# Holding one load of x, one set of output products and one early store in the planner's order of a fused attention and state-space kernel

## The chip, the cores and the metric

The kernel runs on one core of a Trainium2 chip. The metric is device time in microseconds (us) of one execution. Five engines matter: TensorE (PE, with its weight loads shown as PEld), ScalarE (ACT), VectorE (DVE), GpSimd (POOL), and SyncE (SP), which here only issues DMAs.

## The reference

The input x has 2048 rows of 448. Two branches are computed from it and mixed by a gate per row:

```python
x = A_x
g = _sigmoid((x * gate_w).sum(-1, keepdims=True))
a = _A_ref(x, A_wq, A_wk, A_wv, A_wo)
b = _B_ref(x, B_A_re, B_A_im, B_B_re, B_B_im, B_C_re, B_C_im, B_log_dt, B_Dskip)
return g * a + (1 - g) * b
```

Branch A is attention with 16 query heads of 28 and one shared key and value head: scores of 2048 x 2048 per head, softmax, the product with v, and an output product with wo. Branch B is a long convolution of each of the 448 channels with a kernel K of 2048 taps, K being a sum over 256 complex modes, plus a skip term.

## The kernel before, in words

The rows of x are taken as four query chunks of 512 rows, and each chunk's 16 heads as four groups of four heads, so there are 16 items i = 0 to 15 (chunk i // 4, group i % 4). Each item has 16 key tiles times 4 heads, 64 score tiles of 128 x 512; there are 1024 score tiles in all. They are worked on in 410 sets, by turns three tiles and two: `qk` (L1298) puts a set's scores into PSUM banks 0 to 4, either from `qT` with K of 29 rows (L1311) or from the masked copy `qM` with 128 rows (L1334), and ACT takes the exponential of the set in one instruction (L1366) into a ring of tiles `expT`. `pv` multiplies four such tiles with v (L1385) into `psB`, and after 16 key tiles `norm` (L1140) copies the sums to `acc` (L1146), fetches the denominators by three small round trips through POOL's DMA queue (denT, R_scratch, rdenB), and writes the normalised heads to `onT` (L1158).

`qproj(i)` (L860) makes the queries of item i: four matmuls of `xT` with Wq (L870), an absolute maximum on DVE (L876), one more matmul (L879), a copy to `qT` (L882), and four DMAs on POOL's queue to `qM`. `xT` holds one query chunk. After the last group of a chunk, at i = 3, 7 and 11, `qproj` also loads the next chunk of x from the DRAM scratch `XS` into `xT`, 448 KB on POOL's queue. The one at i = 7 brings the third chunk, which `qproj(8)` to `qproj(11)` read.

When a chunk's four groups are normalised, `outp(qc, tt)` (L1122) forms the output products of one of its four tiles of 128 rows: four matmuls with Wo (L1128) into one bank, and `fold` (L1134) adds them, times the gate, to the result `O` on DVE (L1137). qc = 2 is the third chunk.

Branch B runs in the shade of this. `masters` and `tables` build tables of powers on DVE, `kgen(c)` (L1002) for c = 0 to 13 multiplies them into 32 channels of K (L1022), copies them out (L1034) and writes them to the DRAM scratch `KP` by POOL's queue. `tload` brings them back as Toeplitz tiles, about 1.1 MB in four DMAs on SP's queue, into one of five buffers (three in `T`, two in `U` once `U` is used up), and two such loads feed one of the 28 convolutions. `conv(c)` (L1074) has 128 small matmuls, 32 planner operations of four (L1089, kept in `self.cm[c, 0..31]`), a scaling copy (L1099), 16 transposing matmuls (L1110) and an addition into `O` (L1119). `stores` writes the first 320 columns of the first three chunks early, one DMA per chunk on SP's queue.

The order on each engine is not the order of the code. Every operation is given to a planner (`Prog`) with an engine, an assumed duration, its data dependencies and a priority `pr` (smaller goes first: score sets 0, the load of x 1, convolutions 1.6, output products 1.58, query products 1.5). `schedule` (L180 on) is a list scheduler: it keeps a clock per engine, takes at each step the operation that can start first, by priority where times tie, and so fixes each engine's sequence. Output products, convolutions, `kgen` and query products share two PSUM banks (5 in `psS`, and `psX`), handed out as locks. The planner also counts PE's instructions and keeps to a time for the fetching of each block of 256. Its gaps on PE are filled with matmuls that only keep the array busy (L1293).

`pg.after[i] = j` makes operation i wait, in the plan, until j is placed:

```python
for i, d in self.after.items():
    if d not in ops[i].deps:
        need[i] += 1
        succ[d].append(i)
```

It does not enter `deps`, and only `deps` become semaphore waits in `waits` and `emit`. The early stores use this too: `STORES` names three score sets, and store qc is held in the plan until the first scores of its set are placed. After that it still waits, by semaphore, for the four tiles of `O` that it writes out.

Of the kernel before, what the change touches and what calls it, by code (L numbers as in the profile page):

```python
# [44 lines left out]
WARM = 64  # L45
NEWQ = 15
LASTQ = 13
STORES = (338, 341, 362)
EARLY = 20
PAIRS = 3  # L50
OUTB = (None, 4, 1, 2)
# [10 lines left out]
class Buf:  # L62
    def __init__(self, handle):
        self.h = handle
        self.rs = handle[:].ap[0][0]
# [17 lines left out]
def dram(t, off, dims):  # L83
    return bass.AP(tensor=t.tensor, offset=t.offset + off, ap=[list(d) for d in dims])
# [308 lines left out]
def el(n, rate=0.96, fix=68):  # L393
    return fix + n / rate
# [14 lines left out]
class Kernel:  # L409
    def __init__(self, nc, ins, out):  # L410
        self.nc, self.ins, self.out = nc, ins, out
        self.es = ExitStack()

    def sb(self, name, cols, dt):
        return Buf(self.es.enter_context(self.nc.sbuf_tensor(name, [P, cols], dt)))
# [4 lines left out]
    def build(self):  # L420
        nc = self.nc
        with self.es:
            self.pg = Prog(nc, self.es)
            self.alloc()
            self.consts()
            self.loads()
            self.prep_x()
            self.prep_params()
            self.prep_u()
            self.prep_gate()  # L430
            self.main()
            self.pg.schedule()
            with nc.Block() as block:
                self.pg.emit(block)
# [425 lines left out]
    def qproj(self, i):  # L860
        pg = self.pg
        qc, g = i // 4, i % 4
        s = i % 2
        X = ("qx", i)
        G = self.grp()
        px = lambda: G.v(0, P, 0, [[1, 512]])

        pr = 0.2 if i == 0 else 1.45 if i < 4 else 1.5
        for T in range(NT):
            pg.op("pe", lambda e, T=T: e.matmul(  # L870
                px(), self.Wq.v(0, DT, T * 512 + g * 128, [[1, 128]]),
                self.xT.v(0, DT, T * 512, [[1, 512]]), start=(T == 0), stop=(T == 3),
                tile_position=(0, 0), skip_group_check=True), 226,
                rd=["Wq"] + self.xk(0) + (["kap"] if i == 1 else []), wr=[X, ("q", s)], pr=pr, lock=G if T == 0 else None)
        av = self.qT.v(0, P, 512 * s, [[1, 512]])
        pg.op("dve", lambda e: e.tensor_reduce(  # L876
            av, G.v(0, P, 0, [[1, 512], [1, 1]]), AX.X, ALU.max, apply_absolute_value=True), el(512),
            rd=[X], wr=[("q", s)], pr=pr)
        pg.op("pe", lambda e: e.matmul(px(), self.Wb.v(0, P, 0, [[1, P]]), av, start=False, stop=True,  # L879
                                       tile_position=(0, 0), skip_group_check=True), 230,  # L880
              rd=["Wb", ("q", s)], wr=[X], pr=pr)
        o = pg.op("dve", lambda e: e.tensor_copy(self.qT.v(0, P, 512 * s, [[1, 512]]), px()), el(512),  # L882
                  rd=[X], wr=[("q", s)], pr=pr, unlock=G)
        if i == 0:
            self.qc0 = o.i
        if i in (3, 7, 11):
            pg.dma([(self.xT.v(0, DT, 0, [[1, XQ]]), dram(self.XS, qc * DT * XQ, [[XQ, DT], [1, XQ]]))],
                   (112, 4096), "xl", rd=[("XS", qc + 1)], wr=self.xk(0), pr=1, eng="pool", extra=9000)
        if True:
            pg.dma([(self.qM.v(32 * h, 32, s * XQ + 512 * h, [[1, 512]]), self.qT.v(32 * h, 32, 512 * s, [[1, 512]]))  # L890
                    for h in range(4)], (128, 1024), f"qm{s}", rd=[("q", s)], wr=[("qM", s)], pr=0, eng="pool", extra=4500)
# [230 lines left out]
    def outp(self, qc, tt):  # L1122
        pg = self.pg
        X = ("ox", qc, tt)
        G = self.grp()
        px = lambda: G.v(0, P, 0, [[1, D]])
        for g in range(4):
            pg.op("pe", lambda e, g=g: e.matmul(  # L1128
                px(), self.onT.v(0, P, g * 512 + 128 * tt, [[1, 128]]), self.Wo.v(0, P, g * D, [[1, D]]),
                start=(g == 0), stop=(g == 3), tile_position=(0, 0), skip_group_check=True), 200,  # L1130
                rd=["Wo"] + [("on", gg) for gg in range(4)], wr=[X], pr=1.58, lock=G if g == 0 else None)
        self.fold(qc, tt, px, 0, D, [X], unlock=G)

    def fold(self, qc, tt, px, off, n, rd, unlock=None):  # L1134
# [130 lines left out]
    def main(self):  # L1265
# [32 lines left out]
        def qk(s):  # L1298
# [58 lines left out]
            self.prevset = o.i  # L1357
            if s in STORES:
                self.hold.append(o.i)
# [121 lines left out]
```

## Time and profile before

| what | us |
|---|---|
| median of 3 runs | 501.96 (500.3 to 503.63) |
| the profiled execution | 504.37 |
| its span, first to last instruction | 502.6 |
| ACT busy | 484.9 |
| PE busy | 479.3 |
| DVE busy | 455.6 |

The span holds a start of some 22 us, in which x is transposed and the first queries are made, then the 410 exponentials from 21.8 to 495.6 us, and a tail of 7 us for the last products and stores. PE's busy time contains 150 filling matmuls of 385 ns (L1293). All three engines are close to full, so one reads the profile for the places where ACT, the fullest, is idle.

### The profile page before, as it was taken

The numbers are of one execution on the slowest core, as the hardware profiler recorded it, in microseconds if no ns is written. First come the engines' busy times: TensorE is split into PE (matmuls) and PEld (weight loads), VectorE is DVE, ScalarE is ACT, GpSimd is POOL, SyncE is SP. The second block draws the span as 40 slices with busy tenths as digits, with TensorE's granted clock in tenths as the row PEclk, the third lists the DMA queues.
The fourth block names the chain that finished last, engine by engine and source line by source line (L and its number), as shares of the span: only waits on it lengthen the run. The fifth ranks groups of instructions, "written<-read, shape, count | busy, mean of one in ns | idle before, by whom it ended". The sixth has DMA issues, their size and how long they took to land.

```text
span 502.6 us, 17345 instructions
## 1 busy us (share of the span) xinstructions
PE 479.3 (95%) x7643; PEld 210.2 (42%) x7643; DVE 455.6 (91%) x867; ACT 484.9 (96%) x436; POOL 146.3 (29%) x282
## 2 busy tenths in 40 slices
PE   8899999999999999799999999999999999999997
PEld 6432233343443434344343343543534344444453
DVE  6999999999999999899999999999999999896213
ACT  6999999999999999899999999999999999899995
POOL 2102044234143433214306052520513424143110
PEclk9999999999999999999999999999999999899999
DMA  8997695928438566992943951499693776739742
GB/s 243 323 188 186 121 155 131 270 61 256 142 81 269 154 182 112 280 215 42 296 98 52 287 159 65 120 265 320 128 326 48 215 238 186 232 103 306 226 163 69
DMA packets 152423, 91.86 MB, mean 183 GB/s; under 512 B 84538, under 2 KB 148332, under 8 KB 152348
## 3 DMA queue, kind: packets, MB, share of 16 engines
q1 hardware_dynamic: 143370, 81.21, 60.8%
q0 software_dynamic: 8704, 9.41, 7.6%
q8 instruction: 60, 0.98, 0.8%
q14 instruction: 15, 0.12, 0.1%
q10 hardware_dynamic: 274, 0.14, 0.1%
HBM read 73.61 MB, written 5.23 MB: 157 GB/s over the span
## 4 chain that ended last, share of the span: by engine, by line
ACT 81%; PE 10%; DMA 1%; issue 1%; SPq 0%
ACT expT L1366 81%; PE psS L1311 2%; PE psS L1334 2%; DMA T<-KP_scratch 1%; PE psB L1385 1%; PE psS L1089 1%; PE psS L1224 1%; PE psB L1293 1%; PE psX L1022 1%; PE psB L1287 1%; PE psX L1089 0%; SPq L158 0%; PE psS L1022 0%; PE psS L870 0%; PE psX L870 0%
## 5 line engine op out<-in xcount | busy, mean ns | idle before, releaser
L1366 ACT ACTIVATE expT<-psS 128x1536 bf16<-128x1536 f32 (+1 forms) x410 | 465.1, 1390 | 6.3 <-PE psS L1334 3.0
L963 DVE TENSOR_TENSOR tab<-tab,mbf 128x512 bf16<-128x512 bf16 (+4 forms) x140 | 139.5, 1000 | 0.0
L1311 PE MATMUL psS<-qT,kT 29*128 29x512 bf16 x684 | 96.3, 387 | 10.3 <-ACT expT L1366 5.2
L1385 PE MATMUL psB<-expT,vaug 128*32 128x512 bf16 x1000 | 100.5, 392 | 0.1
L1334 PE MATMUL psS<-qM,kT 128*128 128x512 bf16 x316 | 95.4, 385 | 1.5 <-ACT expT L1366 0.4
L158 POOL DMA_DIRECT2D KP_scratch<-kstg x104 | 57.4, 559 | 84.0 <-DVE kstg L1034 76.5
L978 DVE TENSOR_TENSOR tab<-tab 128x256 bf16<-128x256 bf16 (+4 forms) x140 | 76.9, 574 | 0.0
L1385 PEld LDWEIGHTS psB<-expT,vaug 128*32 128x32 bf16 x1000 | 25.6, 93 | 73.3 <-issue 71.5
L158 POOL DMA_DIRECT2D qM<-qT x64 | 32.4, 513 | 61.7 <-DVE qT L882 39.9
L1311 PEld LDWEIGHTS psS<-qT,kT 29*128 29x128 bf16 x684 | 23.7, 91 | 63.6 <-ACT expT L1366 49.3
L1293 PE MATMUL psB<-ident,one 128*128 128x512 bf16 x150 | 48.8, 385 | 0.0
L158 POOL DMA_DIRECT2D rdenB<-R_scratch x60 | 30.9, 520 | 51.3 <-DMA R_scratch<-denT 51.1
L1089 PE MATMUL psS<-T,U 128*26 128x128 bf16 (+3 forms) x1792 | 40.0, 223 | 0.9 <-DMA T<-KP_scratch 0.9
L1089 PEld LDWEIGHTS psS<-T,U 128*26 128x26 bf16 (+3 forms) x1792 | 30.9, 106 | 14.7 <-issue 9.2
L1089 PE MATMUL psX<-T,U 128*32 128x128 bf16 (+3 forms) x1472 | 34.4, 222 | 2.2 <-issue 2.2
L158 POOL DMA_DIRECT2D denT<-acc x15 | 10.8, 718 | 88.0 <-DVE acc L1146 88.0
L992 DVE TENSOR_TENSOR tab<-tab,tmp 128x1984 bf16<-128x1984 bf16 x28 | 32.3, 1186 | 0.1
L1089 PEld LDWEIGHTS psX<-T,U 128*32 128x32 bf16 (+3 forms) x1472 | 25.8, 106 | 15.8 <-issue 11.3
L1334 PEld LDWEIGHTS psS<-qM,kT 128*128 128x128 bf16 x316 | 19.0, 97 | 28.2 <-ACT expT L1366 19.1
L986 DVE TENSOR_TENSOR tmp<-tmp,mq 128x64 bf16<-128x64 bf16 (+4 forms) x70 | 25.5, 365 | 0.1
L909 DVE TENSOR_TENSOR msq<-seedz 128x512 f32<-128x512 f32 (+1 forms) x40 | 24.6, 615 | 0.0
L1022 PE MATMUL psX<-tab 128*64 128x128 bf16 x544 | 22.6, 224 | 1.3 <-issue 1.0
(187 smaller groups left out, 483.8 us busy)
## 6 DMA issues: line engine op xcount, KB each, us to landing
T<-KP_scratch SPq DMA_DIRECT2D x204, 272.0 KB, 5.2
U<-KP_scratch SPq DMA_DIRECT2D x20, 272.0 KB, 5.5
rdenB<-R_scratch POOLq DMA_DIRECT2D x60, 64.0 KB, 3.7
U<-cst SPq DMA_DIRECT2D x1, 3584.0 KB, 23.8
qM<-qT POOLq DMA_DIRECT2D x64, 32.0 KB, 3.8
tab<-in_A_x_dram SPq DMA_DIRECT2D x4, 448.0 KB, 5.5
O<-in_A_x_dram SPq DMA_DIRECT2D x16, 112.0 KB, 4.6
O<-cst SPq DMA_DIRECT2D x1, 1792.0 KB, 9.5
```

The lines of the kernel that those rows point to most:

```text
L158: return [e.dma_start(o, i, **kw) for o, i in pairs]
L963: mul = lambda e, o, a, b: e.tensor_tensor(o, a, b, ALU.mult)
L978: vo(lambda e, dv=dv, tv=tv, k=k: e.tensor_tensor(dv, dv, tv, ALU.add if k else ALU.subtract), n, [kt[k], kd[k]], [kd[k]], 1.92 if lv else ...
L986: vo(lambda e, w=w, lv=lv: e.tensor_tensor(rho.v(0, P, (32 - 2 * w) * 2, [[64, 32], [2, w], [1, 2]]), rho.v(0, P, (32 - w) * 2, [[64, 32], ...
L992: vo(lambda e, k=k: e.tensor_tensor(tab.v(0, P, FM + k * FP + 2, [[64, 32], [2, 31], [1, 2]]), tab.v(0, P, lm + k * PL + 62, [[64, 32], [- ...
L1022: r = e.matmul(G.v(64 * u, 64, 128 * k, [[1, 128]]), tab.v(0, P, lo + comp * PL + cg * 64 + u, [[2, 64]]), tab.v(0, P, fo, [[64, 2], [mo - ...
L1089: r = e.matmul(ps.v(32 * j, 32 - m0, 128 * k, [[1, 128]]), self.U.v(0, P, (4 * gi + j) % UA // 2 * 128 + 2 * (2 * m0 + par) + j % 2, [[4, ...
L1293: return e.matmul(t.v(0, P, off, [[1, 512]]), self.one.v(0, P, 2, [[0, P]]), self.ident.v(0, P, 0, [[0, 4], [1, P]]), start=b != 6, stop=b ...
L1311: r = e.matmul(self.psS.v(0, P, 512 * b, [[1, 512]]), kT.v(32 * h, DH + 1, 128 * kt, [[1, 128]]), qT.v(32 * h, DH + 1, 512 * (i % 2), [[1, ...
L1334: return e.matmul(self.psS.v(0, P, 512 * b, [[1, 512]]), kT.v(0, P, 128 * kt, [[1, 128]]), self.qM.v(0, P, (i % 2) * XQ + 512 * h, [[1, 51 ...
L1366: o = pg.op("act", lambda e: e.activation(expT.v(0, P, 512 * es[0], spread(es, n)), self.psS.v(0, P, 512 * bs[0], spread(bs, n)), AF.Exp, ...
L1385: r = e.matmul(self.psB.v(32 * h, 32, 0, [[1, 512]]), vaug.v(0, P, 32 * kt, [[1, 32]]), expT.v(0, P, 512 * ring[t], [[1, 512]]), start=(kt ...
```

## The change

Three things are held later in the plan. The load of the third chunk of x is not placed before the first operation of convolution 9. The first matmul of each of the four output products of the third chunk (and with it the three that follow) is not placed before the last operation of convolution 21. The third early store is tied to score set 366 and not 362. The two holds are noted in a list while the operations are made, as the operations of the convolutions don't exist yet, and go into `pg.after` just ahead of `schedule`. No instruction is added or removed by the text of the change; the planner works its order out anew.

```diff
-STORES = (338, 341, 362)
+STORES = (338, 341, 366)
...
     def __init__(self, nc, ins, out):
         self.nc, self.ins, self.out = nc, ins, out
         self.es = ExitStack()
+        self.held = []
...
             self.main()
+            for i, c in self.held:
+                self.pg.after[i] = self.cm[c]
             self.pg.schedule()
...
         if i in (3, 7, 11):
             pg.dma([(self.xT.v(0, DT, 0, [[1, XQ]]), dram(self.XS, qc * DT * XQ, [[XQ, DT], [1, XQ]]))],
                    (112, 4096), "xl", rd=[("XS", qc + 1)], wr=self.xk(0), pr=1, eng="pool", extra=9000)
+            if i == 7:
+                self.held.append((pg.ops[-1].i, (9, 0)))
...
                 rd=["Wo"] + [("on", gg) for gg in range(4)], wr=[X], pr=1.58, lock=G if g == 0 else None)
+            if qc == 2 and g == 0:
+                self.held.append((pg.ops[-1].i, (21, 31)))
         self.fold(qc, tt, px, 0, D, [X], unlock=G)
```

## The prediction

> **What bounds the kernel now.** I read the page of the profile first (busy shares, the chain that ended last, the DMA queues), then the windows of 12.56 us for where ScalarE is not full, then the timeline of those windows, then the landings of the loads of T.
>
> ```profile
> span 502.6 us, 17345 instructions
> PE 479.3 (95%) x7643; PEld 210.2 (42%) x7643; DVE 455.6 (91%) x867; ACT 484.9 (96%) x436; POOL 146.3 (29%) x282
> q8 instruction: 60, 0.98, 0.8%
> ACT 81%; PE 10%; DMA 1%; issue 1%; SPq 0%
> ```
>
> ScalarE's exponentials (ACT) are 81% of the chain, so what leaves ACT idle in the main loop is what can be gained. The windows (columns: window, length, then busy time and count for PE, PEld, DVE, ACT, POOL; granted clock, DMA share, GB/s) show where that is:
>
> ```profile
> 201.00:213.60 12.60, 9.66 (x205) 4.04 (x192) 10.22 (x16) 10.44 (x10) 3.27 (x6) 0.93 0.95 280
> 213.60:226.20 12.60, 12.47 (x285) 6.08 (x283) 11.52 (x22) 11.75 (x11) 1.99 (x4) 0.94 0.92 215
> 226.20:238.70 12.50, 12.33 (x208) 5.79 (x207) 12.50 (x32) 12.50 (x12) 5.28 (x9) 1.00 0.23 41
> ...
> 339.30:351.80 12.50, 11.54 (x208) 4.75 (x206) 11.32 (x23) 11.82 (x11) 0.72 (x1) 1.00 1.06 320
> ...
> 427.20:439.80 12.60, 11.45 (x245) 5.70 (x233) 10.84 (x26) 11.29 (x11) 1.74 (x4) 0.89 0.78 231
> 439.80:452.30 12.50, 12.40 (x245) 6.06 (x243) 11.87 (x16) 11.97 (x12) 5.09 (x9) 0.97 0.36 102
> ```
>
> ACT idles 2.16 + 0.85 = 3.01 us at 201 to 226, 0.68 at 339 to 352, 1.31 + 0.53 = 1.84 at 427 to 452: 5.53 us in all. Elsewhere between 75 and 490 it is full. DVE idles in the same three places, so its long chain moves up with them. The timeline of the first and third place:
>
> ```profile
> 200.30 0.56 POOL L158 DMA_DIRECT2D xT<-XS_scratch  x1 [2.01 <-PE psS L1089]
> 208.53 0.41 PE L1089 MATMUL psX<-T,U 128*26 128x128 bf16 x15
> 211.15 0.49 PE L1089 MATMUL psX<-T,U 128*30 128x128 bf16 x21 [2.20 <-issue]
> 212.50 1.02 ACT L1366 ACTIVATE expT<-psS 128x1024 bf16<-128x1024 f32 x1 [2.09 <-PE psS L1334]
> ...
> 427.31 2.55 SPq L158 DMA_DIRECT2D U<-KP_scratch  x4
> 430.33 2.60 SPq L158 DMA_DIRECT2D T<-KP_scratch  x4
> 432.98 0.60 SPq L158 DMA_DIRECT2D out_dram<-O  x1
> 434.77 0.31 PE L1022 MATMUL psX<-tab 128*64 128x128 bf16 x4
> 436.08 0.31 PE L1022 MATMUL psX<-tab 128*64 128x128 bf16 x4 [1.01 <-issue]
> ```
>
> Both PE gaps lie inside a group of matmuls and no semaphore ends them ("issue"). The trace's DMA packets name the cause: queue 8 carries 60 packets of 16,384 B, one per about 256 PE instructions, that is PE's own code. One began at 208.49 and took 1.14 us; PE went on 1.5 us after it landed (211.15 against 209.63). Another began at 433.60, landed at 434.74, and PE went on at 436.08. Counted in PE's instruction records (a fetch comes after 254 of them in the mean) these two were due at 205.2 and 429.2, so they waited 3.3 and 4.4 us before they began; by that count they are the two latest of the 60. In both cases loads of T filled the DMA engines (280 GB/s at 201 to 213). After both gaps the clock records show half clock for 3.41 us, which doubles the harm.
>
> A rule speaks against this reading: the Trainium skill, "Runtime: NRT & Kernel Launch", section "Instruction fetch mechanics", says that code is prefetched in 16 KiB blocks and that this is mostly hidden. The trace agrees on the size and differs on the hiding in 2 of 60 cases. By that rule the gaps are something else, the change would leave them, and the time is 502.0. That is rival 2.
>
> **The load of x, third chunk.** One DMA on POOL's queue (0.56 us there), 448 KB, whose 4096 B packets ran from 202.9 to 204.6, right ahead of the late fetch. It moves behind the planner's time for convolution 9, whose first matmul ran at 222.4. The hold orders the plan and puts no semaphore in the program, so on the chip the load goes when POOL gets there: after the four rdenB issues that end at 218.5, ahead of the KP write at 231.7. POOL is idle in between (13.2 us), so its own 0.56 us costs nothing, and the KP writes behind it wait for DVE (230.74) anyway; without that cover they would be 0.56 us later.
> - What it removes: 448 KB at 280 GB/s is 1.6 us of the queue ahead of the fetch. The fetch would begin at 206.9, land at 208.0, and PE could go on at 209.5; it ran dry at 208.94. A gap of 0.6 us is left. Gaps of 0.52 and 0.63 us stand at 172.4 and 379.2, and ACT is full there (12.60 of 12.60) with clock 1.00, so I take the whole 3.0 us as gained. Bounds: 0 (the fetch stays behind the T stream alone) to 3.0.
> - What it adds: 1.6 us of traffic at 218 to 226. The T load issued at 217.49 landed at 225.0 and is used at 231.2, so 1.6 us is hidden; without that cover it costs up to 1.6. The load itself lands 5.6 us after issue (8.3 at most), by 231 even if issued at 222.4, and the query products that read it start at 235.66. Their result is first needed at score set 205, that is 21.8 + 205 x 1.154 = 258 us. Hidden.
>
> **The output products of the third chunk.** 16 matmuls of 0.36 us and 4 folds on DVE of 0.68, now from 416.79 to 426.65, ahead of convolution 21 (424.84 to 430.34). They are the same work afterwards, so their sum is 0; the order changes. The T data of convolution 21 were issued by 403.3 and land 4 to 5 us later, by 408, so it can take the free bank at 416.8 and end near 422, with the products at 422 to 432 and convolution 22 behind them, at 430 as now.
> - Now convolution 21 and half of 22 run as 192 matmuls in 7 us, the stretch whose code fetch was late. Afterwards the products, with a quarter of the instructions, lie between the two. Two of the T loads (427.31, 430.33) get their buffers some 8 us earlier and so the four issued from 417.8 on, 4.4 MB at 280 GB/s, should have drained by 433.4. I take the 1.84 us as gained.
> - Bounds: gain 1.84; loss 3.0, the price of the first gap, because four T loads then follow each other from 417.8 on, as four do from 196.6 to 212, where a gap arose. I take the gain, as conv 21 alone is 256 PE instructions, one fetch, in place of 384.
> - Half the clock after a gap is a term of its own: the Trainium skill, "TensorE: Matmul & The Clock Gate", section "What's actually happening", says that the clock halves after an idle window of about 3.4 us. The trace shows the 3.41 us length, but after a gap of 1.01 us. By the page neither gap would halve it, the gain would be at most their length, 2.2 + 1.0, and the time 498.8. As the records show the half clock after both gaps, I give that no chance of its own; the sum goes by ACT's rows.
>
> **The third early store.** One SP issue of 0.60 us, 328 KB in 640 B packets (436.5 to 439), four sets of 1.154 us later: 432.98 becomes 437.6. Behind it on SP comes nothing until 446.53. DMA share is 0.36 there. Cost 0; without the cover, 328 KB at 300 GB/s, 1.1 us, on the next T load. It had no part in the gap: the late fetch began before its packets.
>
> **The sum.** Profiled execution 504.37 (span 502.6 and 1.77 around it), gain 3.01 + 1.84 = 4.85, gives 499.5. The median of the runs is 501.96, 2.4 below the profiled one; the same gain from it gives 497.1, which is my forecast.
>
> **Rivals.**
> 1. One gap stays or another opens (for: five of the other 58 fetches are nearly as late by the same count, and the order after 200 us is planned anew; against: those five cost nothing). It takes back 1.84 to 3.01: 499 to 500.1.
> 2. Nothing gained: the gaps come with the T stream alone, or are no fetches. 502.0. Against: the packets' times.
> 3. Slower: convolution 21 doesn't move up. The products, 9.9 us, then sit behind 430.3 with both free banks, and the table products at 434.8 and convolution 22 are pushed with all that follows up to convolution 27, whose fold ends at 493.07 against its reader at 497.03: 4 us of slack. 9.9 - 4 gives 5.9: 507.9. It decides once the first matmul of convolution 21 is later than about 421. Against: its T lay ready 16 us before.
> 4. A new wait for T, as the 0.9 us at 343, where T landed 0.04 us before its use: 0.9 us alone, or up to twice the 3.0 us of the first gap if it halves the clock: 503 to 508.
> 5. More than forecast: the gap at 339 to 352, a wait for T behind the DMA stream, goes with the new order: 0.68 more, 496.4.
>
> **How the numbers follow.** Forecast 0.30 (its own range 496.3 to 498.3), rival 5 0.22, rival 1 0.22, rival 2 0.10, rival 3 0.10, rival 4 0.06. About 1% (5.0 us) is what a measurement here can tell from no change: below 496.94 is faster, above 506.98 slower. Faster: all of rival 5 and 0.13 of the forecast, which stands on the line, 0.35. Slower: rival 3 and 0.02 of rival 4, 0.12. Within: 0.53. The range goes from 495.0 to 503.0 and leaves out 0.04 below and 0.14 above.
>
> **What would show it.** Right: no PE gap over 1 us with "issue" near 209 and 435, granted clock 1.00 throughout, ACT full at 201 to 226 and 427 to 452, x's third load on POOL between 218 and 231, and convolution 21 ending by 423. Wrong: an "issue" gap at another place with a late queue 8 packet ahead of it, T landing after its use in convolutions 9 or 22, or the same 5.5 us of ACT idle.

## The result and the profile after

Side by side, 20 runs of each kernel gave a median of 499.96 us for the changed one (498.8 to 502.49) and 502.31 for the one before (499.32 to 508.62), a ratio of 0.9951 [0.9929, 0.9973]: 0.5% faster, within the 1% called the same here. (The ratios here and below leave out single executions over 1.5% above the fastest of the same kernel; medians and counts take all.) The forecast was 497.1, 4.9 below the median shown before; measured are 2.4. The two profiled executions differ by much more than the medians: 504.37 before, 499.53 after, so 4.84. How that fits together is what the experiments had to find out.

The changed kernel's page, the four lines that answer to those of before (the new plan has two filling matmuls fewer):

```profile
span 497.8 us, 17345 instructions
PE 476.5 (96%) x7641; PEld 208.2 (42%) x7641; DVE 455.1 (91%) x867; ACT 484.2 (97%) x436; POOL 146.2 (29%) x282
q8 instruction: 60, 0.98, 0.8%
ACT 86%; PE 7%; DMA 2%; issue 0%; SPq 0%
```

Its windows (same columns as before: window, length, then PE, PEld, DVE, ACT, POOL, granted clock, DMA share, GB/s):

```profile
201.00:213.60 12.60, 11.13 (x271) 5.50 (x271) 11.46 (x17) 11.84 (x11) 3.25 (x6) 1.00 0.90 237
213.60:226.20 12.60, 12.33 (x229) 5.24 (x226) 12.56 (x29) 12.60 (x12) 2.52 (x5) 1.00 1.00 237
...
339.30:351.80 12.50, 12.01 (x276) 6.53 (x277) 10.78 (x28) 11.63 (x11) 2.70 (x5) 1.00 0.94 238
...
427.20:439.80 12.60, 12.54 (x187) 5.35 (x184) 12.55 (x29) 12.60 (x12) 5.06 (x9) 1.00 0.49 144
439.80:452.30 12.50, 11.80 (x318) 6.07 (x317) 12.50 (x16) 12.50 (x12) 4.11 (x9) 1.00 0.81 249
```

ACT's idle time fell from 3.01 to 0.76 us at 201 to 226 and from 1.84 to nothing at 427 to 452; at 339 to 352 it is 0.87 (0.68 before). The clock column reads 1.00 in each. From 60 us to its last exponential ACT is idle 2.21 us (430.73 less 428.52) where it was 6.00: 3.79 of the pair's 4.84. The other 1.05 is not shown to be work of the change: 0.41 lies in the first 60 us, ahead of everything that moved (the first score set's exponential starts at 21.30 instead of 21.75), and 0.64 in ACT's instructions, which ran a little shorter.

The timeline of the changed kernel at the places that were changed:

```profile
208.13 0.41 PE L1094 MATMUL psX<-T,U 128*26 128x128 bf16 x15
209.51 0.49 PE L1094 MATMUL psX<-T,U 128*30 128x128 bf16 x21 [0.96 <-issue]
218.21 0.55 POOL L158 DMA_DIRECT2D xT<-XS_scratch  x1
...
420.75 0.68 DVE L1104 TENSOR_TENSOR cst<-psX,omq 128x512 bf16<-128x512 f32 x1
...
432.24 0.36 PE L1133 MATMUL psS<-Wo,onT 128*128 128x448 bf16 x1
```

The load of x went out at 218.21, after the rdenB issues. The gap near 209 is 0.96 us instead of 2.20, its fetch began at 207.03 and landed at 208.18. The scaling copy of convolution 21 came at 420.75 (430.34 before) and the products ran from 419.99 to 432.6; there is no gap near 435. Up to here the shape is what the prediction described. Two things came later than it said: convolution 22 began at 437.69 (430 foretold), and the third store went out at 453.34 (437.6 foretold). The open question is how much of it the change did.

### The profile page after: what moved, and what is told of

It reads as the page before. It is cut to its first block, busy times and chain, and to the rows that moved or that the text cites. A ratio compares the mean times of both kernels' runs of the same rounds, so it can differ in the third digit from the quotient of the medians.

```text
span 497.8 us, 17345 instructions
## 1 busy us (share of the span) xinstructions
PE 476.5 (96%) x7641; PEld 208.2 (42%) x7641; DVE 455.1 (91%) x867; ACT 484.2 (97%) x436; POOL 146.2 (29%) x282
## 4 chain that ended last, share of the span: by engine, by line
ACT 86%; PE 7%; DMA 2%; issue 0%; SPq 0%
ACT expT L1373 85%; DMA T<-KP_scratch 2%; PE psS L1341 1%; PE psS L1318 1%; PE psB L1392 1%; PE psB L1294 1%; PE psS L1231 1%; PE psX L1094 0%; PE psS L1094 0%; SPq L158 0%; PE psB L1300 0%; PE psS L1027 0%; PE psS L873 0%; PE psB L1386 0%; PE psX L1027 0%
## 5 line engine op out<-in xcount | busy, mean ns | idle before, releaser
L1094 PE MATMUL psX<-T,U 128*26 128x128 bf16 (+3 forms) x1728 | 38.6, 221 | 1.2 <-issue 1.0
L1094 PE MATMUL psS<-T,U 128*26 128x128 bf16 (+3 forms) x1536 | 35.6, 221 | 1.1 <-DMA T<-KP_scratch 1.1
L1094 PEld LDWEIGHTS psX<-T,U 128*26 128x26 bf16 (+3 forms) x1728 | 29.6, 105 | 15.0 <-issue 10.0
L1094 PEld LDWEIGHTS psS<-T,U 128*26 128x26 bf16 (+3 forms) x1536 | 27.3, 105 | 13.3 <-issue 7.6
L1300 PEld LDWEIGHTS psB<-ident,one 128*128 128x128 bf16 x148 | 13.3, 97 | 22.1 <-issue 14.4
```

The source lines that it names most:

```text
L1094: r = e.matmul(ps.v(32 * j, 32 - m0, 128 * k, [[1, 128]]), self.U.v(0, P, (4 * gi + j) % UA // 2 * 128 + 2 * (2 * m0 + par) + j % 2, [[4, ...
L1300: return e.matmul(t.v(0, P, off, [[1, 512]]), self.one.v(0, P, 2, [[0, P]]), self.ident.v(0, P, 0, [[0, 4], [1, P]]), start=b != 6, stop=b ...
```

## Theories

The theory of the prediction is that the load's 448 KB stand ahead of PE's code in the DMA engines, so that taking them away shortens the wait, and that moving the products does the same near 435. The first rival is that the code is late through the whole T stream and by chance, with the load's bytes no part of it. The second is that the gain comes from the new order elsewhere, the load's place being only what started the replanning. E1, E4 and E5 take the change apart; E6, E10 and E12 change the load's size and leave its place; E13 and E14 cross the load's place with the order of everything else; E7 and E8 look for a better version. With the store's edit alone the planner gives the order of before, so that kernel was not run.

## What the runs have in common: stretches of half clock

Most runs list their mean granted clock. One stretch of 3.41 us at half clock lowers the mean over 500 us by 0.0034, so 0.997, 0.993 and 0.990 mean one, two and three stretches. Sorted so, all runs of the two unedited kernels that list a clock (from several chips) give:

| stretches in a run | before: runs, median us | after: runs, median us |
|---|---|---|
| none | 20, 499.9 | 27, 499.8 |
| one | 36, 502.2 | 6, 502.0 |
| two | 34, 504.3 | 1, 503.9 |
| three | 7, 505.8 | none |
| four or more | 5, 506.6 | none |
| mean over all | 1.43 stretches, 502.95 | 0.24 stretches, 500.32 |

Without a stretch the two kernels take the same time. The first two cost (504.3 - 499.9) / 2 = 2.2 us each, and 1.19 fewer at 2.2 us is 2.6 us, the difference of the two means (2.63). So by this count the whole gain is rarer half clock, together with the pauses that bring it on. On the one chip that ran both kernels with clocks listed it is the same: 1.29 stretches per run before (31 runs) and 0.21 after (14). The profiled execution of before had two stretches, one more than the middle of its runs; that of after had none, as most of its runs.

A stretch follows a quiet PE. In all traces stretches start a whole number of 3.413 us apart, so the clock is decided in slots of that length, and the slot before a stretch always has PE partly idle. The windows of before, laid on these slots:

```profile
208.35:211.76 3.41, 1.21 (x40) 0.68 (x38) 1.03 (x2) 2.07 (x2) 0.00 (x0) 1.00 1.07 297
211.76:215.17 3.41, 3.41 (x31) 0.96 (x30) 2.93 (x3) 2.06 (x2) 0.57 (x1) 0.50 0.67 194
433.63:437.04 3.41, 2.26 (x47) 1.20 (x49) 3.41 (x9) 2.98 (x4) 0.00 (x0) 1.00 1.07 361
437.04:440.45 3.41, 3.41 (x63) 1.79 (x61) 1.65 (x3) 2.53 (x3) 0.26 (x1) 0.50 0.24 76
```

PE was busy 1.21 and 2.26 of 3.41 us, and the next slot reads 0.50. Over the traces, busy shares of 0.35 to 0.71 were followed by half clock and some of 0.62 to 0.73 were not, so PE's busy share is not quite what is counted. The Trainium skill, "TensorE: Matmul & The Clock Gate", section "What's actually happening", has a window of 3413 ns that runs on its own, not from the kernel's start, and half clock after an idle window. The length and the free running agree with the traces; the idleness does not, as a slot with PE two thirds busy was enough. Since the slots lie differently in each execution, a gap of 0.6 to 1 us halves the clock in some executions of one PE order only; the five gaps of 1.8 us and more that were seen did so each time.

## The change taken apart: E1, E4, E5

Four kernels ran side by side on one chip (before: 503.21, 35 runs; the others 12 runs each), E6 of the next section among them.

**E1, the load of x alone.**

```diff
-STORES = (338, 341, 366)
+STORES = (338, 341, 362)
-            if qc == 2 and g == 0:
+            if qc == -2 and g == 0:
```

> The load of x for the third chunk is held behind convolution 9; the output products and the third store stay as before. My theory (two late fetches of PE code, each with bytes ahead of it on the DMA engines, and a half clock after a gap only in some executions): the PE gap near 209 shrinks from 2.20 us to about 1.0, the gap near 435 stays about 1.0 (its surroundings are planned anew, so it may wander by some us); median 0.2 to 0.4% below before, ratio 0.996 to 0.998. Rival A (the whole gain is this load): ratio 0.995. Rival B (the load has nothing to do with it, the gain is the later order): 1.000.

Measured 503.99, ratio 1.0024 [0.9992, 1.0057]: no gain. The gap near 209 is 1.04 us and no half clock follows it; ACT's last exponential ends at 491.37, 4.2 us ahead of before. Yet the span is 501.9. E1's timeline at the end:

```profile
486.18 5.19 ACT L1373 ACTIVATE expT<-psS 128x1024 bf16<-128x1024 f32 x5
...
493.95 0.85 PE L1094 MATMUL psS<-U 128*28 128x128 bf16 x48
...
496.76 0.55 PE L1237 MATMUL psS<-O,ident 128*128 128x448 bf16 x2 [0.53 <-DVE O L1124]
497.16 0.98 ACT L1254 ACTIVATE O<-psS 128x448 bf16<-128x448 f32 x2 [5.78 <-PE psS L1237]
```

The same place in the changed kernel:

```profile
485.30 5.43 ACT L1373 ACTIVATE expT<-psS 128x1024 bf16<-128x1024 f32 x5
...
487.81 0.42 DVE L1124 TENSOR_TENSOR O<-O,psS 128x256 bf16<-128x256 bf16 x1 [0.68 <-PE psS L1115]
...
492.57 0.54 ACT L1254 ACTIVATE O<-psS 128x448 bf16<-128x448 f32 x1 [1.84 <-PE psS L1237]
```

In E1 the plan leaves 48 matmuls of convolution 27 for after the last scores; its fold ends 5.3 us after the last exponential, and ACT's final copy waits 5.78 us. In the changed kernel that fold ends 2.5 us before the last exponential (488.23 against 490.73). So the held load alone spoils the end of the plan, and what it saves is spent there: without half clock E1 takes 503.4, 3.6 us more than the changed kernel.

**E5, the load and the products, the store as before.**

```diff
-STORES = (338, 341, 366)
+STORES = (338, 341, 362)
```

> The change without its third part: the store stays tied to set 362, all else as in the changed kernel. PE, DVE, ACT and POOL then have the changed kernel's order, and only SP's sequence differs. My theory: the store had no part in the gap near 435, ratio 0.995 as for the whole change, within 0.1%. Rival (the store's place matters, as it waits on SP for the moved products and what is behind it on SP waits too): the T loads for convolution 23 are issued after the last fold of the products, some us later than 425 to 427, and the ratio is 0.997 to 1.002.

Measured 500.07, ratio 0.9944 [0.991, 0.9978]: the changed kernel's time without the store's edit. The store left at 434.42, and the next issue on SP came at 440.74. Against E1, on the same chip, the held products are worth 3.9 us, and by the lines above that is the tail, not a fetch.

**E4, the products and the store, the load as before.**

```diff
-            if i == 7:
+            if i == -7:
```

> The output products of the third chunk are behind convolution 21 and the third store is tied to set 366; the load of x is where it was. My theory: the gap near 209 stays at about 2.2 us, with half clock after it in many executions; no gap of 1 us between 415 and 450; ratio 0.997 to 0.999. Rival A (all from the load of x): 1.000, with the gap near 435 still there. Rival B: 0.995.

Measured 501.85, ratio 0.9971 [0.9939, 1.0004], with 1.0 stretches per run. The gap near 209 is there with its half clock (timeline of E4):

```profile
212.72 0.49 PE L1094 MATMUL psX<-T,U 128*30 128x128 bf16 x21 [2.07 <-issue]
```

Near 435 there is no gap. E4's other stretch, at 57.3, follows a place that the change does not touch: there PE waited 0.95 us for a copy on DVE. Up to 416.8 E4's order on PE is that of before. By the medians of E4 and E5 the load's hold is the larger part of the gain, and only together with the products (E1); but the two intervals overlap, so the shares are not shown.

## Is it the load's bytes? E6, E12, E10

**E6 and E12: the order of before, an eighth of the load's bytes** (the rest of the chunk is left unloaded, so the outputs of those rows are not the reference's). E6 cuts the third chunk's load; E12, run beside E7, E8 and E10 on another chip (before: 502.68, 35 runs), cuts the fourth too (`i >= 7`).

```diff
+            nx = XQ // 8 if i == 7 else XQ
-            pg.dma([(self.xT.v(0, DT, 0, [[1, XQ]]), dram(self.XS, qc * DT * XQ, [[XQ, DT], [1, XQ]]))],
+            pg.dma([(self.xT.v(0, DT, 0, [[1, nx]]), dram(self.XS, qc * DT * XQ, [[XQ, DT], [1, nx]]))],
```

> The kernel before, with the program's order unchanged on every engine, but the load of x for the third chunk moves one eighth of each row (56 KB and not 448), so the queries of the third chunk are made from mostly old data: part of the computation is left out. My theory: bytes ahead of the code fetch are what makes it late; the gap near 209 shrinks from 2.20 to about 1.0 us, as it did when the load was moved, and the gap near 435 stays; ratio 0.996 to 0.998, the same as for the load moved alone. Rival B (the order and not the bytes): the gap near 209 stays at 2.2 us and the ratio is 1.000.

> The kernel before, order unchanged, with the loads of x for the third and the fourth chunk both cut to one eighth of each row (the queries of these chunks are then made from mostly old data: part of the computation is left out). My theory: besides the gap near 209, which shrinks to 1 us or less as with the third alone, the waits for T between 335 and 346 lose up to 1.6 us, the time that 448 KB take; median 0.3 to 1 us below that of the kernel with the third load alone cut, so a ratio of 0.993 to 0.996. Rival: the waits near 340 come from the T loads alone and stay, ratio 0.9955.

E6: 500.54, ratio 0.9955 [0.9917, 0.9993]. E12: 501.92, ratio 0.9982 [0.9948, 1.0016]. E6 looked like proof of the theory, and E12 took it away: with the same PE order up to there and the same small load its gap is 1.89 us, with half clock behind it. E6 and then E12 in their timelines:

```profile
209.16 0.49 PE L1089 MATMUL psX<-T,U 128*30 128x128 bf16 x21 [0.77 <-issue]
```

```profile
210.39 0.50 PE L1089 MATMUL psX<-T,U 128*30 128x128 bf16 x21 [1.89 <-issue]
```

E12 also waits 1.62 us for T at 342.7, so the wait near 340 is not due to the fourth load either.

**E10: the order of before, twice the bytes** (a second copy of 448 KB from DRAM to DRAM in the same issue; nothing reads it). The scratch is made larger for the copy, and the planner's issue time per DMA is halved for this one, so that the plan stays as it was.

```diff
+            more = [(dram(self.XS, 3 * DT * XQ, [[XQ, DT], [1, XQ]]), dram(self.XS, qc * DT * XQ, [[XQ, DT], [1, XQ]]))] if i == 7 else []
-            pg.dma([(self.xT.v(0, DT, 0, [[1, XQ]]), dram(self.XS, qc * DT * XQ, [[XQ, DT], [1, XQ]]))],
+            pg.dma([(self.xT.v(0, DT, 0, [[1, XQ]]), dram(self.XS, qc * DT * XQ, [[XQ, DT], [1, XQ]]))] + more,
```

> The kernel before, same order on PE, DVE, ACT and SP, with a second copy of the same 448 KB beside the load of x for the third chunk: one more DMA on POOL's queue, from the DRAM scratch into an unused part of it (0.56 us more of POOL, which is idle there). My theory (bytes ahead of the code fetch): the gap near 209 grows from 2.2 us to 3.5 us or more, it halves the clock in nearly every execution, and the ratio is 1.003 to 1.008. Rival (the gap comes from the T loads and the order, and one eighth of the load made it smaller by chance): the gap stays at 2.2 us within 0.4 and the ratio is 1.000 to 1.002.

Measured 502.23, ratio 0.999 [0.9961, 1.0019], and the gap near 209 is gone; E10's timeline there and further on:

```profile
208.65 0.49 PE L1089 MATMUL psX<-T,U 128*30 128x128 bf16 x21 [0.22 <-issue]
...
375.68 0.39 PE L1311 MATMUL psS<-qT,kT 29*128 29x512 bf16 x3 [0.63 <-ACT expT L1366]
...
379.35 1.45 ACT L1366 ACTIVATE expT<-psS 128x1536 bf16<-128x1536 f32 x1 [0.55 <-PE psS L1311]
```

The copy's packets ran from 203.5 to 206.9 and the code fetch began at 206.17, so the added bytes did lie ahead of it. Twice the bytes and the shortest gap: the theory's step from the load's bytes to the gap's length falls. The lines at 375 and 379 show something that the prediction had passed over. In the order of before PE waits there for ACT with nothing else to do, which looks harmless, as ACT is full. E10's windows, on the slots:

```profile
370.53:373.94 3.41, 3.41 (x60) 1.40 (x60) 3.41 (x5) 3.41 (x4) 0.00 (x0) 1.00 0.92 245
373.94:377.36 3.42, 2.43 (x36) 0.89 (x36) 3.42 (x6) 3.42 (x4) 0.97 (x2) 1.00 0.49 51
377.36:380.77 3.41, 3.41 (x73) 1.87 (x73) 3.41 (x14) 2.86 (x3) 1.84 (x4) 0.50 0.59 84
```

PE is quiet for 0.99 of 3.42 us while ACT is full. In the next slot the clock is halved, PE becomes the slower engine, and ACT loses 0.55 us at once. This pause (0.63 us; 0.96 in E4 and E6, whose traces lack one matmul's record there) is in every profile of the order of before, in E4 and in E8, and was followed by half clock in E8, E10 and E12. It is in no other profile with the load held in the plan: the replanned order does not have it.

## The same kernels looked at again

The size runs left open how much the gap near 209 varies by itself, so both unedited kernels were profiled twice more.

> The kernel before, unedited, for a second profile of it. Up to the gap near 209 the order on PE, DVE and ACT is one and the same with and without the held load, so differences there are the load's or chance. Theory 1 (the load ahead of the fetch decides): a gap near 209 of 1.8 us or more again, a half clock right after it. Theory 2 (how late a fetch is, is chance in each execution, and the order only sets the odds): the gap is anywhere from 0 to 2.2 us, as it was 0.77, 1.89 and none in the three runs that had this order with another size of load.

> The kernel before, unedited, a third profile. As for the second: theory 1 gives 1.8 us or more near 209, theory 2 anything from 0 to 2.2. The gap near 435 is about 1 us by theory 1, and by theory 2 present or not.

> The changed kernel, unedited, for a second profile. In the four profiles with the load held so far the gap near 209 was 0.66 to 1.04 us and no half clock followed. Theory 1: again 0.6 to 1.1 us. Theory 2: anything from 0 to 2.2 us.

> The changed kernel, unedited, a third profile. Theory 1: 0.6 to 1.1 us near 209 and no half clock there. Theory 2: anything from 0 to 2.2 us.

The table has every profile whose PE order is that of before up to the gap (E8's is not).

| load of x | gaps near 209, us |
|---|---|
| old place, full size | 2.20 (before), 1.81 and 1.32 (before again), 2.07 (E4), 1.38 (E14) |
| old place, an eighth | 0.77 (E6), 1.89 (E12) |
| old place, doubled | 0.22 (E10) |
| moved | 0.96 (after), 1.34, 0.28 and 1.25 (after again), 1.04 (E1), 0.66 (E5), 0.83 (E7), 0.83 (E13) |

The two executions of before took 499.66 (gap 1.32, mean clock 1.000) and 502.23 (gap 1.81, clock 0.997); neither has a gap over 0.2 us near 435. Those of after took 499.92 and 500.64, clocks 1.000 and 0.999, no stretch. With one program the fetch began 2.7 to 3.6 us after convolution 7 started (before, three profiles; after, four: 2.0 to 2.9). The gap near 435 stood in before (1.01), E10 (0.73) and E12 (1.06), while the two repeats, E6 and E13 have at most 0.42 there, with the same order on PE; so the prediction had read a feature of one execution as one of the kernel.

Where the half clock lay can be counted too. The seven profiles of the order of before (three of before, E6, E10, E12, E13) have seven full stretches: three behind the gap near 209, two behind the pause at 376 to 380, one behind the gap near 435, and one (E13) at 58.9, where PE had waited 1.61 us for a copy on DVE as in E4. The six profiles of the changed order (four of after, E5, E14) have none ahead of their last exponential. Their order lacks the pause and the gap near 435, and still has the gap near 209.

## The load's place or the order: E13, E14

Both kernels leave all other engines' sequences alone and move only the load of x on POOL, after planning: E13 to its late place in the order of before, E14 to its early place in the order of the changed kernel. They ran with the changed kernel on one chip (before: 502.76, 28 runs).

```diff
             self.pg.schedule()
+            L = self.pg.lists["pool"]
+            k = [j for j, x in enumerate(L) if x[0].slot == "xl"][1]
+            e = L.pop(k)
+            d = [j for j, x in enumerate(L) if x[0].slot == "rdb" and j >= k][0]
+            L.insert(d + 1, e)
```

(E13; E14 puts it back ahead of the last "dn" issue before it, with its waits worked out anew.)

> The kernel before with one edit after the planning: in POOL's sequence the load of x for the third chunk is taken out of its place ahead of the denT DMA and put behind the rdenB DMAs, where the changed kernel has it. PE, DVE, ACT and SP keep the order of before to the last instruction. Theory 1 (where this load lies decides how late the code fetch near 208 is): the gap near 209 is 0 to 1.4 us, half clocks are rarer than in before (about 1.5 a run so far), ratio 0.995 to 0.998. Theory 2 (the later order on PE sets the odds of half clocks): 0.999 to 1.001, half clocks as often as in before.

> The changed kernel with one edit after the planning: in POOL's sequence the load of x for the third chunk is put back to its old place, ahead of the denT DMA; PE, DVE, ACT and SP keep the changed order. Theory 1: the gap near 209 is 1.3 to 2.2 us again, mostly with a half clock behind it, so about one half clock a run and a ratio to before of 0.997 to 1.000. Theory 2: 0.995, with half clocks as rare as in the changed kernel (5 in 20 runs).

> The changed kernel, unedited, beside the two above on the same chip, so that the four corners (load early or late, order of before or changed) stand in one table. Both theories: 0.993 to 0.997.

| | load early | load late |
|---|---|---|
| order of before | 502.76; 1.43 stretches per run (102 runs, all chips) | E13: 501.66, 0.9982 [0.9944, 1.0019]; 0.83 (12 runs) |
| order of the changed kernel | E14: 501.1, 0.9959 [0.993, 0.9989]; 0.42 (12 runs) | 499.82, 0.9966 [0.9935, 0.9996]; 0.24 (34 runs) |

Each step goes the right way, but the order (1.43 to 0.42, 0.83 to 0.24) does more than the load's place (1.43 to 0.83, 0.42 to 0.24), and with E13's interval the place alone is not shown to gain. The counts behind E13 and E14 are small, 10 and 5 stretches. Against calling the load harmless stands that all three kernels with the order of before and little or no load ahead of the fetch have fewer stretches than before (E6 0.75, E12 1.00, E13 0.83; 31 in 36 runs together), and for it that E10, with twice the load, has 1.17 and not more than before. The second rival holds best: with the load early in both, the order alone gains (E14, whose interval leaves out 1). What can be seen to differ are the pause at 376 to 380 and the gap near 435, which it no longer has. E4, which has lost the gap near 435 and keeps the pause, is at 1.00 (12 runs); no run takes away the pause alone, so the share of each is not shown.

## Looking for a better version: E7, E8

**E7: the fourth load of x held too**, behind the first operation of convolution 16.

```diff
-            if i == 7:
-                self.held.append((pg.ops[-1].i, (9, 0)))
+            if i >= 7:
+                self.held.append((pg.ops[-1].i, (9, 0) if i == 7 else (16, 0)))
```

> The changed kernel with one more hold: the load of x for the fourth chunk is not placed before the first operation of convolution 16. My theory: the 0.95 us that ACT still loses between 327 and 352 goes, and the number of executions with a half clock stays as low as in the changed kernel; ratio to before 0.993 to 0.995. Rival (each new order brings its own late fetches or a longer tail): 0.995 or more, with a gap of 1 us at a new place.

Measured 503.02, ratio 1.001 [0.9979, 1.0042]: nothing of the gain is left. Its timeline:

```profile
343.59 1.80 PE L1094 MATMUL psS<-T,U 128*32 128x128 bf16 x60 [1.64 <-DMA T<-KP_scratch]
```

PE waits 1.64 us for T, the clock halves at 343.45, and ACT's next exponential comes after 2.89 us of idle time.

**E8: the planner's time for a fetch 5000 ns instead of 4800**, all holds kept.

```diff
-    BLOCK, FIRST, FETCH, IDLE, NEED, QUIET = 256, 158, 4800.0, 3300.0, 0.015, 480000.0
+    BLOCK, FIRST, FETCH, IDLE, NEED, QUIET = 256, 158, 5000.0, 3300.0, 0.015, 480000.0
```

> The changed kernel with the planner's allowance for the fetch of a block of PE code raised from 4800 to 5000 ns, which makes it spread the convolutions a little more; nothing else is edited. My theory: late fetches are what is left near 208, so the gap there shrinks from 0.96 to about 0.7 us and half clocks become rarer still; ratio to before 0.993 to 0.996. Rival (the order is so full that any new allowance is paid back in the tail): the last convolution ends later against the last exponential than the 2.5 us before it that the changed kernel has, ratio 0.997 or more.

Measured 502.79, ratio 0.9992 [0.9966, 1.0017], 1.08 stretches per run. The quiet place moved to another convolution, now as a wait for T:

```profile
224.67 0.36 PE L1094 MATMUL psX<-T,U 128*32 128x128 bf16 x12 [1.86 <-DMA T<-KP_scratch]
```

Half clock follows at 226.38, and again at 379.98 behind the pause that this order has once more. No version here beat the changed kernel.

## Where the prediction was right and where it failed

- **Where the time is lost: right for the profiled pair.** ACT's idle stretches, PE's gaps and the half clock behind them are where the changed kernel's execution gains on that of before. The pause at 376 to 380, which halved the clock in other executions, was passed over.
- **The failing step: "the same gain from it gives 497.1".** The sum for the profiled execution was 4.85 and the pair of profiles gave 4.84, an agreement that is partly luck: 1.05 of it is not shown to be the change's (above). The prediction then took all of it off the median. But 4.85 is about the price of two half-clock stretches, and the median run of before has one: 36 of 102 runs have one and 34 two. Runs of before without a stretch were at 499.9 already, so taking away all half clock brings the median to about 499.9, and no run of either unedited kernel was below 498.3. What the median could gain is thus one stretch of 2.2 us, and 2.35 were measured. Ahead of the forecast only three other times of before were known, with no clocks, but their spread (500.3 to 503.63) already said that an execution of this kernel could take 4 us less than the profiled one without any change.
- **The load's term, 3.01: mechanism not borne out, size 2.25 in the profiled pair.** "448 KB at 280 GB/s is 1.6 us of the queue ahead of the fetch" fails: with double the bytes the gap was 0.22, with an eighth 1.89. The trace of before spoke against it too: the load's last packet ended at 205.2 (the prediction read 204.6), 3.3 us ahead of the fetch that it was to delay. A smaller gap after a moved load is seen (0.28 to 1.34 against 1.32 to 2.20), but why is open. Its cover was as said: issued at 218.21 in POOL's idle time, and no wait for T behind it cost ACT anything at 213.6 to 226.2.
- **The products' term, 1.84: wrong cause.** The gap that they were to remove is absent or below 0.5 us in four of seven profiles of that order. What they earn is the tail that the held load would otherwise spoil (3.9 us, E5 against E1). Convolution 21 moved up as foretold (420.75 against "near 422"). Convolution 22 did not stay at 430, and the two T loads were issued 5 us earlier (422.29, 425.33), not 8; neither cost ACT anything, as it is full there.
- **The store's term, 0: right** (E5), though the store went out 16 us later than foretold.
- **Rivals.** Rival 1's time (499 to 500.1) is nearest, though a stretch that stays is not the reason. Rival 2's time did not come, but half of its cause, a gap near 209 that stays whatever this load does, fits E10, E12 and the repeats better than the prediction's. Rival 3 had the right place and the wrong cause: branch B came too late at the end when the products were not held (E1). Rival 4's wait for T came in E7 and E8, not in the changed kernel. In rival 5 the wait at 339 to 352 stayed (0.87).

Open are three things: why a fetch in the same order begins 2.7 to 3.6 us after convolution 7 does; whether the load's place alone matters; and what exactly is counted when the clock is granted.

## What to carry to other kernels

Before a gain read from one profiled execution is taken off a median, see how typical that execution is: the mean granted clock of each run gives the number of half-clock stretches, here 2.2 us each, and the runs without any show the floor that removing them can reach. A short pause of PE in the shade of a full engine is not free if it halves the clock of the next slot; giving such a place some matmuls is the thing to try next (no run here did). When a planner makes the order anew, compare the tail and the pauses of the whole program, not only the place that was edited: E1 lost at 494 what it won at 209.

## What was not expected of the hardware

Half clock was granted after slots in which PE was still 35 to 71% busy, on a grid of 3.413 us whose phase differs from execution to execution; so identical programs ran at 499.7 and 502.2 us. And the wait of a code fetch did not follow the bytes put ahead of it: over all profiles in the table the gap near 209 ran from 0.22 to 2.20 us with the same PE instructions ahead of it.
